# Attention and two expert layers: the second layer gathers quarter rows, and VectorE turns them in 32x32 blocks

## The chip, the cores and the metric

The kernel runs on one core of one Trainium2 chip. The metric is device time in microseconds (us) of one execution, as the median of three runs. TensorE (PE in the views) does the matrix products, VectorE (DVE), ScalarE (ACT) and GpSimd (POOL) the rest; SyncE (SP) issues most plain transfers, GpSimd issues the indirect ones (gathers and scatters by a table of row numbers).

## The reference

Three stages follow each other on N = 2304 tokens of D = 512 values: attention (4 batches, 8 heads, 576 positions, 64 values per head), a mixture of experts where each token goes to one of 8 experts, and a second one where each token goes to two. The second is the stage that is changed:

```python
def _moe2_ref(x, w_gate, w_noise, noise, w1, w2):
    logits = x @ w_gate
    noisy_logits = logits + np.log1p(np.exp(x @ w_noise)) * noise
    top2 = np.argpartition(-noisy_logits, 2, axis=1)[:, :2]
    ...                                  # top2_w: softmax over the two
    for e in range(E):                   # E = 8, w1[e] 512x1024, w2[e] 1024x512
        for k in range(2):
            mask = top2[:, k] == e
            out[mask] += top2_w[mask, k, None] * (np.maximum(x[mask] @ w1[e], 0.0) @ w2[e])
```

## The kernel before

Every fp32 product is made as three products of a rounded high part and a low part (high by high, high by low, low by high), so each matrix that is multiplied is first split: ScalarE casts the high part, VectorE subtracts it to get the low part. Attention and the first expert layer are put in order by a planner (queue `Q`); their last part and the second layer are written out in program order, which each engine follows.

**Layer 1 hands over through DRAM.** `x1_out` (line 871) writes each finished pair of 128-row blocks of layer 1's output to the table `xd` (520 values per row, 8 of them for routing). A few rows per expert that stay empty are filled with zeros during attention (`M.later`, line 1104).

**Layer 2** (`layer2`, line 967) begins at about 508 us. Each expert has 640 slots, in five tiles of 128 (the first 32 slots are always empty). Expert 0's first two tiles are done early, beside the end of the routing; its other three and then experts 1 to 7 follow, one expert per turn of the loop:

- *mm1* (lines 718 to 720): 8 blocks of hidden columns, each in two groups of 12 matmuls on 304 slots. ScalarE and VectorE turn each group into `hh` and `hl` (lines 721, 723), from two PSUM banks that alternate. In the same stretch `split_w` (693, 694) splits this expert's `w2`.
- *mm2* (lines 728 to 730): five output tiles, each in two half-calls of 12 matmuls with 512 columns. Between half-calls a list `todo` is worked off two entries at a time: eight splits of the next expert's `w1` (`split_w1`, 697, 698) and the five tiles of the next expert's input (`xsplit`, 705 to 710). `xsplit` turns a gathered tile with four TensorE transposes (708) into PSUM, casts `xh` from there (709) and subtracts for `xl` (710).
- *output* (`l2_out`, line 960): ScalarE scales the tile into `os` (963; two buffers that alternate), and a GpSimd scatter adds its rows to `out` in DRAM (964). Each scatter waits until the one before has landed, since both write `out`; ScalarE may write an `os` buffer again only when the scatter from it has landed.
- *loads*: at the top of an expert GpSimd issues five gathers of 128 rows of `xd` for the next expert (701, five buffers `gs`). SyncE loads the next `w2` when mm1 is over, and the `w1` after next when the last `split_w1` is done (690); each load is 2 MB.

Of the kernel before, what the change touches and what calls it, by code (L numbers as in the profile page):

```python
# [307 lines left out]
class Moe:  # L308
    def __init__(s, ctx, tc, ident, consts, areas):
# [40 lines left out]
    def blocks(s, nc, c, areas):  # L350

        def T(j, o, w, name, dt=FT):
            assert o+w<=AREAS[j]
# [4 lines left out]
        s.w1r=V(T(K0,0,4096,'w1r'),KD); s.w2r=V(T(K0,4096,4096,'w2r'),KF); s.os=cut(K0,8192,512,'os',2)
        s.w1h=V(T(K1,0,4096,'w1h',FR),KD); s.w1l=V(T(K1,4096,4096,'w1l',FR),KD); s.yt=V(T(K1,8192,1024,'yt'),KD); s.rr=c.tile([128,4,256],FR,name='rrm')
        s.xh=V(T(X,0,2560,'xh',FR),KD); s.xl=V(T(X,2560,2560,'xl',FR),KD)  # L360
        s.w2h=cut(W2,0,512,'w2h',KF,FR); s.w2l=cut(W2,4096,512,'w2l',KF,FR)
# [3 lines left out]
        s.wb1=V(T(W2,0,4096,'wb1'),KD); s.wb2=V(T(W2,4096,4096,'wb2'),KF)  # L365
        s.x1=V(T(X1,0,2*XW,'x1'),2); s.ol2=V(T(OL,0,512,'ol2',FR),4); s.gs=cut(G,0,XW,'gs',GB); s.gn_=s.on_=0
# [593 lines left out]
    def l2_out(s, wk, y, tb, c, out):  # L960
# [3 lines left out]
        nc.gpsimd.indirect_dma_start(out=out,out_offset=bass.IndirectOffsetOnAxis(ap=si[:,c:c+1],axis=0),in_=o,in_offset=None,compute_op=OP.add)  # L964
    def l2_gather(s, wk, tb, c, ts=range(T2)):
        return [s.gather(s.xd[:],tb[0][:,c+t:c+t+1]) for t in ts]
    def layer2(s, w1, w2, out):
# [7 lines left out]
        s.load_w(s.w1r,w1,E+1)  # L975
        s.chain=s.route2(wk,ps,NF+NP2,2); s.hold=0
        for f in range(KF):
            s.mm1(ps,f,DEAD,EARLY-DEAD)
            if f==1: s.behind()
            if f in LSLOT2: s.logits(wk,ps,1+LSLOT2.index(f))  # L980
            s.split_w(s.w2r,s.w2h,s.w2l,f,nc.vector if f in (3,5,7) else nc.gpsimd)
            if f>LSLOT2[2]: s.pump(f,GATE2,PUMP2)
        s.load_w(s.w2r,w2,E+1)
        for t in range(NE):
# [15 lines left out]
        for e in range(E):  # L1000
            nxt=e+1<E
            if nxt:
                if e: s.load_w(s.w1r,w1,E+e+1)
                g=s.l2_gather(wk,tb,(e+1)*TS)
            for f in range(KF):
# [8 lines left out]
            for t in range(T2): todo.insert(2*t+1,lambda t=t:s.xsplit(ps,g[t],t*128))
            n=-(-len(todo)//(2*len(ts)-1))
            for t in ts:
                for q in range(2):
                    y=s.mm2(ps,t*128,range(4*q,4*q+4),y if q else None)
                    if nxt:
                        for _ in range(n):  # L1020
                            if todo: todo.pop(0)()
# [55 lines left out]
def build(tc, q, k, v, mz, beta, ids, mbias, wg, w1, w2, wcat, noise, out):  # L1077
    nc = tc.nc
    with ExitStack() as ctx:
# [24 lines left out]
        M.later = [Q.add(100 * (5 + j // 5), SP, 1000, f, [A.sunk[4 + j // 5]]) for j, f in enumerate(dma)]  # L1104
# [51 lines left out]
```

## Time and profile before

| | us |
|---|---|
| median of three runs | 985.74 |
| lowest and highest run | 985.54, 986.47 |
| the profiled execution | 987.47 |
| span of its trace | 985.8 |
| TensorE busy | 946.3 |
| VectorE busy | 541.9 |
| ScalarE busy | 487.4 |
| GpSimd busy | 350.4 |

The profiled execution is one more run of the same program, so sums made from its rows start from 987.47, of which 1.67 lie outside the span. Busy shares are averages over three unlike stages; a stage's own rows say what limits it.

### The profile page before, as it was taken

The numbers are of one execution on the slowest core, as the hardware profiler recorded it, in microseconds if no ns is written. First come the engines' busy times: TensorE is split into PE (matmuls) and PEld (weight loads), VectorE is DVE, ScalarE is ACT, GpSimd is POOL, SyncE is SP. The second block draws the span as 40 slices with busy tenths as digits, with TensorE's granted clock in tenths as the row PEclk, the third lists the DMA queues.
The fourth block names the chain that finished last, engine by engine and source line by source line (L and its number), as shares of the span: only waits on it lengthen the run. The fifth ranks groups of instructions, "written<-read, shape, count | busy, mean of one in ns | idle before, by whom it ended". The sixth has DMA issues, their size and how long they took to land. (4 is left out here: it accounts for less than half of the span.)

```text
span 985.8 us, 18580 instructions
## 1 busy us (share of the span) xinstructions
PE 946.3 (96%) x6849; PEld 832.9 (84%) x6849; DVE 541.9 (55%) x1695; ACT 487.4 (49%) x1141; POOL 350.4 (36%) x411
## 2 busy tenths in 40 slices
PE   7999999999998999999988999999999999999994
PEld 5888888878875989888877999898989989898983
DVE  8777777888764667777755244243342424244310
ACT  6887878775433555555543243343342333334320
POOL 5222232244543667766744231121314021221111
PEclk9999999999999999999989999999999999999997
DMA  8336856261485655556654253536446354534212
GB/s 210 109 103 187 272 180 201 101 222 53 173 274 221 215 198 189 195 196 211 214 189 137 65 134 124 128 76 161 109 107 164 105 120 117 150 77 110 30 20 37
DMA packets 83841, 144.98 MB, mean 147 GB/s; under 512 B 14480, under 2 KB 32912, under 8 KB 83728
## 3 DMA queue, kind: packets, MB, share of 16 engines
q1 hardware_dynamic: 73168, 117.10, 36.1%
q0 software_dynamic: 10560, 26.47, 13.5%
q8 instruction: 60, 0.98, 0.4%
q14 instruction: 53, 0.43, 0.1%
HBM read 111.65 MB, written 31.97 MB: 146 GB/s over the span
## 5 line engine op out<-in xcount | busy, mean ns | idle before, releaser
L718 PE MATMUL b<-xh,w1h 128*128 128x304 f32 (+3 forms) x800 | 241.8, 302 | 6.2 <-ACTq L791 3.7
L719 PE MATMUL b<-xl,w1h 128*128 128x304 f32 (+3 forms) x800 | 239.4, 299 | 3.3 <-DVEq L786 3.1
L720 PE MATMUL b<-xh,w1l 128*128 128x304 f32 (+3 forms) x800 | 238.5, 298 | 0.0
L723 DVE SCALAR_TENSOR_TENSOR hl<-b,hh 128x304 fp32r<-128x304 f32 (+3 forms) x200 | 90.9, 454 | 232.7 <-ACT hh L721 227.2
L728 PE MATMUL b<-w2h,hh 128*128 128x512 f32 x464 | 187.8, 405 | 0.0
L730 PE MATMUL b<-w2h,hl 128*128 128x512 f32 x464 | 181.7, 392 | 0.0
L729 PE MATMUL b<-w2l,hh 128*128 128x512 f32 x464 | 181.0, 390 | 0.0
L964 POOL DMA_INDIRECT out_dram<-os,l2s x40 | 63.1, 1578 | 329.3 <-ACT os L963 256.2
L721 ACT ACTIVATE hh<-b 128x304 fp32r<-128x304 f32 (+3 forms) x200 | 81.8, 409 | 182.6 <-PE b L720 172.2
L718 PEld LDWEIGHTS b<-xh,w1h 128*128 128x128 f32 x800 | 154.1, 193 | 13.2 <-DVE hl L723 5.5
L719 PEld LDWEIGHTS b<-xl,w1h 128*128 128x128 f32 x800 | 154.3, 193 | 4.4 <-DVEq L786 3.3
L720 PEld LDWEIGHTS b<-xh,w1l 128*128 128x128 f32 x800 | 154.3, 193 | 0.0
L730 PEld LDWEIGHTS b<-w2h,hl 128*128 128x128 f32 x464 | 87.1, 188 | 19.5
L729 PEld LDWEIGHTS b<-w2l,hh 128*128 128x128 f32 x464 | 87.4, 188 | 15.6
L728 PEld LDWEIGHTS b<-w2h,hh 128*128 128x128 f32 x464 | 87.2, 188 | 15.4
L151 ACT ACTIVATE p<-sm,l 128x128 f32<-128x128 f32 (+4 forms) x144 | 84.1, 592 | 16.9 <-DVE l L147 16.9
L698 DVE TENSOR_TENSOR w1l<-w1r,w1h 128x512 fp32r<-128x512 f32 x84 | 67.9, 816 | 23.7 <-ACT w1h L697 23.5
L693 ACT CAST w2h<-w2r 128x512 fp32r<-128x512 f32 x128 | 78.5, 613 | 0.0
L710 DVE TENSOR_TENSOR xl<-b,xh 128x512 fp32r<-128x512 f32 x56 | 38.6, 689 | 71.9 <-ACT xh L709 71.9
L709 ACT CAST xh<-b 128x512 fp32r<-128x512 f32 x56 | 32.9, 587 | 89.6 <-PE b L708 89.5
L963 ACT ACTIVATE os<-b,l2w 128x512 f32<-128x512 f32 x40 | 27.7, 691 | 97.8 <-PE b L730 47.9
L697 ACT CAST w1h<-w1r 128x512 fp32r<-128x512 f32 x128 | 74.8, 620 | 0.0
(457 smaller groups left out, 1497.6 us busy)
## 6 DMA issues: line engine op xcount, KB each, us to landing
w1r<-in_w_dram SPq DMA_DIRECT2D x18, 2048.0 KB, 9.5
w2r<-in_w_dram SPq DMA_DIRECT2D x18, 2048.0 KB, 9.1
xd<-gs SPq DMA_DIRECT2D x24, 260.0 KB, 3.1
xd<-x SPq DMA_DIRECT2D x10, 520.0 KB, 10.8
out_dram<-gs SPq DMA_DIRECT2D x19, 256.0 KB, 2.6
k<-in_k_dram SPq DMA_DIRECT2D x16, 256.0 KB, 3.9
q<-in_q_dram SPq DMA_DIRECT2D x16, 256.0 KB, 3.2
v<-in_v_dram SPq DMA_DIRECT2D x16, 256.0 KB, 5.4
```

The lines of the kernel that those rows point to most:

```text
L151: s.nc.scalar.activation(s.P[b,i,u][:,lh*n:lh*n+n],s.SM[b,i,u][:,lh*n:lh*n+n],AF.Exp,scale=-1.0,bias=L[:,0,c:c+1],accum_out=L[:,1,c:c+1])
L693: nc.scalar.copy(hi[c],raw[:,c])
L697: nc.scalar.copy(s.w1h[:,:,fs],s.w1r[:,:,fs])
L698: eng.tensor_sub(s.w1l[:,:,fs],s.w1r[:,:,fs],s.w1h[:,:,fs].bitcast(FT))
L718: nc.tensor.matmul(h[:,:n],s.w1h[:,k,fs],s.xh[:,k,cs],start=k==0,stop=False)
L719: nc.tensor.matmul(h[:,:n],s.w1h[:,k,fs],s.xl[:,k,cs],start=False,stop=False)
L720: nc.tensor.matmul(h[:,:n],s.w1l[:,k,fs],s.xh[:,k,cs],start=False,stop=k==KD-1)
L721: def mm1_a(s, h, f, c0, n): s.nc.scalar.activation(s.hh[:,f,c0:c0+n],h[:,:n],AF.Relu)
L723: cs=slice(c0,c0+n); s.nc.vector.scalar_tensor_tensor(s.hl[:,f,cs],h[:,:n],0.0,s.hh[:,f,cs].bitcast(FT),op0=OP.max,op1=OP.subtract)
L728: nc.tensor.matmul(y,s.hh[:,f,cs],s.w2h[f],start=f==0,stop=False)
L729: nc.tensor.matmul(y,s.hh[:,f,cs],s.w2l[f],start=False,stop=False)
L730: nc.tensor.matmul(y,s.hl[:,f,cs],s.w2h[f],start=False,stop=f==KF-1)
```

## The change

Layer 1 writes its output twice: to `xd` as before, and to a new table `xq` that holds each row as four quarter rows of 128 values (512 bytes). The zero rows are written to `xq` too, 24 more transfers.

In layer 2, experts 1 to 7 fetch each tile with four gathers of 128 quarter rows instead of one gather of 128 whole rows, 140 gathers where there were 35. The four gathers place the quarters so that 32x32 blocks of one tile are all that has to be transposed: one VectorE block transpose (`bsplit`) turns it in SBUF, ScalarE casts from there, VectorE subtracts. The order of the 512 values that the product sums over becomes another, and `w1` of these experts is loaded in that order (`by='(p c)'`: 16 KB in one piece per partition, where it was four of 4 KB). The gathers are no longer issued together: those of tile 0 stand at the top of an expert, the others each behind a one-column copy (`pace`) that reads a result of mm1 (`hl`) or of a split (`w1l`). The order of the list `todo` changes too. A table of quarter row numbers is worked out once (`quarter_sel` on GpSimd, `quarter_tables` with four small matmuls and two VectorE steps). Expert 0 keeps whole rows and TensorE transposes.

```diff
+    def bsplit(s, g, c0):
+        nc=s.nc; x=s.xt_[s.xn%2]; s.xn+=1
+        nc.vector.transpose(x.rearrange('p j (s t) -> p s j t',s=4),g.rearrange('p (s d j) -> p s j d',s=4,j=KD))
+        nc.scalar.copy(s.xh[:,:,c0:c0+128],x)
+        nc.vector.tensor_sub(s.xl[:,:,c0:c0+128],x,s.xh[:,:,c0:c0+128].bitcast(FT))
...
-        s.nc.sync.dma_start(d[:,c:c+n] if isinstance(c,int) else d[:,bass.ds(c,n)],s.x1[:,:n])
+        for d,w in ((d,XW),(dq,D)): s.nc.sync.dma_start(d[:,c:c+n] if isinstance(c,int) else d[:,bass.ds(c,n)],s.x1[:,:n,:w])
...
+    def quarter_gather(s, c, t, behind=None):
+        if behind is not None: s.nc.gpsimd.tensor_copy(s.pace,behind.bitcast(FT))
+        for i in range(4):
+            s.nc.gpsimd.indirect_dma_start(out=s.gq[t][:,i*128:(i+1)*128],out_offset=None,in_=s.xq[:],in_offset=bass.IndirectOffsetOnAxis(ap=s.gq4[:,i,c+t:c+t+1],axis=0))
...
+            if f==5: s.quarter_sel()
...
+        s.quarter_tables()
         for t in range(NE,T2): s.xsplit(ps,ge[t-NE],t*128)
...
-                if e: s.load_w(s.w1r,w1,E+e+1)
-                g=s.l2_gather(wk,tb,(e+1)*TS)
+                if e: s.load_w(s.w1r,w1,E+e+1,by='(p c)')
+                s.quarter_gather((e+1)*TS,0)
...
+                at=(2,4,6) if not e else (3,6)
+                if nxt and f in at: s.quarter_gather((e+1)*TS,1+at.index(f),s.hl[:,f,C2-1:C2])
...
-            for t in range(T2): todo.insert(2*t+1,lambda t=t:s.xsplit(ps,g[t],t*128))
+            for t in range(T2): todo.insert(2*t+2 if t<4 else len(todo),lambda t=t:s.bsplit(s.gq[t],t*128))
+            later=[(0,4)] if not e else [(0,3),(2,4)]
...
+                        i=2*(t-ts[0])+q
+                        if later and i==later[0][0]: s.quarter_gather((e+1)*TS,later.pop(0)[1],s.w1l[:,0,(i+1)*128:(i+1)*128+1])
...
-        M.later = [Q.add(100 * (5 + j // 5), SP, 1000, f, [A.sunk[4 + j // 5]]) for j, f in enumerate(dma)]
+            dma.append(lambda r=r: nc.sync.dma_start(M.xq[4 * (r - N):4 * (r - N) + 512].rearrange('(p q) d -> p (q d)', q=4), zt[:, :D]))
+        M.later = [Q.add(100 * (5 + j // 7), SP, 1000, f, [A.sunk[4 + j // 7]]) for j, f in enumerate(dma)]
```

**GpSimd's order** around the mm2 of expert 1, before: the five gathers for expert 2 (`gs`) stand together at the top, and behind them expert 1's five scatters (`os`).

```order
L701 DMA gs_98<-xd,l2g 128x520
L701 DMA gs_99<-xd,l2g 128x520
L701 DMA gs_100<-xd,l2g 128x520
L701 DMA gs_96<-xd,l2g 128x520
L701 DMA gs_97<-xd,l2g 128x520
L964 DMA out_dram<-os_61,l2s 2432x512
L964 DMA out_dram<-os_62,l2s 2432x512
L964 DMA out_dram<-os_61,l2s 2432x512
```

The same piece of the changed kernel, from the gathers of tile 0 to the second scatter.

```order
L992 DMA gq_94<-xq,gq_8406 128x128 x4
L990 COPY pace<-hl_88 128x1
L992 DMA gq_95<-xq,gq_8406 128x128 x4
L990 COPY pace<-hl_88 128x1
L992 DMA gq_96<-xq,gq_8406 128x128 x4
L990 COPY pace<-w1l 128x1
L992 DMA gq_97<-xq,gq_8406 128x128 x4
L973 DMA out_dram<-os_61,l2s 2432x512
L990 COPY pace<-w1l 128x1
L992 DMA gq_98<-xq,gq_8406 128x128 x4
L973 DMA out_dram<-os_62,l2s 2432x512
```

Twenty gathers stand where five stood; those of tile 3 now stand ahead of the first scatter, and those of tile 4 ahead of the second.

**ScalarE's order** in the same mm2 from the first output tile (`os_61`, tile 0) to the last, before: the last cast of a `w1` piece stands behind the third `os`.

```order
L963 ACTIVATE os_61<-b_158,l2w 128x512
L697 CAST w1h<-w1r 128x4x128
L709 CAST xh<-b_159 128x4x128
L697 CAST w1h<-w1r 128x4x128
L709 CAST xh<-b_160 128x4x128
L963 ACTIVATE os_62<-b_157,l2w 128x512
L697 CAST w1h<-w1r 128x4x128
L709 CAST xh<-b_159 128x4x128
L697 CAST w1h<-w1r 128x4x128 x2
L963 ACTIVATE os_61<-b_158,l2w 128x512
L697 CAST w1h<-w1r 128x4x128
L963 ACTIVATE os_62<-b_157,l2w 128x512
```

The same piece of the changed kernel; `xtq` is the tile that VectorE has turned.

```order
L972 ACTIVATE os_61<-b_167,l2w 128x512
L711 CAST xh<-xtq_99 128x4x128
L699 CAST w1h<-w1r 128x4x128
L711 CAST xh<-xtq_100 128x4x128
L699 CAST w1h<-w1r 128x4x128
L972 ACTIVATE os_62<-b_166,l2w 128x512
L711 CAST xh<-xtq_99 128x4x128
L699 CAST w1h<-w1r 128x4x128 x3
L972 ACTIVATE os_61<-b_167,l2w 128x512
L711 CAST xh<-xtq_100 128x4x128
L972 ACTIVATE os_62<-b_166,l2w 128x512
L972 ACTIVATE os_61<-b_167,l2w 128x512
```

The last `w1` cast has moved ahead of the third `os` (it stood behind it), and the casts of the x tiles no longer read a PSUM bank that TensorE wrote.

**TensorE's order** at the first gap between half-calls of that mm2, before: the four transposes of a tile (`ident`, `gs`) stand between two half-calls. Five such rows per expert are gone from the changed kernel, 35 in all.

```order
L728 MATMUL b_158<-w2h_72,hh_87 128x512
L729 MATMUL b_158<-w2l_80,hh_87 128x512
L730 MATMUL b_158<-w2h_72,hl_88 128x512
L708 MATMUL b_159<-ident,gs_98 128x128 x4
L728 MATMUL b_158<-w2h_73,hh_87 128x512
```

In the changed kernel the last row follows the third directly.

## Rows read from the trace of the kernel before

**Rows 1.** The page's first part: busy time, share of the span, instructions.

```profile
PE 946.3 (96%) x6849; PEld 832.9 (84%) x6849; DVE 541.9 (55%) x1695; ACT 487.4 (49%) x1141; POOL 350.4 (36%) x411
```

**Rows 2.** Windows: length, PE, PEld, DVE, ACT, POOL busy, PEclk, DMA share, GB/s.

```profile
750.00:800.00 50.00, 50.00 (x304) 45.75 (x303) 21.77 (x37) 19.78 (x41) 11.80 (x10) 1.00 0.44 99
...
135.00:145.00 10.00, 10.00 (x111) 7.99 (x109) 7.62 (x30) 8.31 (x22) 3.01 (x3) 1.00 1.04 369
```

**Rows 3.** Timeline of TensorE, 662 to 720: start, length, what [idle before it].

```profile
662.39 0.39 PE L728 MATMUL b<-w2h,hh 128*128 128x512 f32 x1
...
678.35 0.47 PE L728 MATMUL b<-w2h,hh 128*128 128x512 f32 x1
...
692.06 0.30 PE L718 MATMUL b<-xh,w1h 128*128 128x304 f32 x1
...
719.43 0.39 PE L728 MATMUL b<-w2h,hh 128*128 128x512 f32 x1
```

**Rows 4.** Groups by line, 530 to 986: busy, mean ns | idle before, releasers.

```profile
L964 POOL DMA_INDIRECT out_dram<-os,l2s x40 | 63.1, 1578 | 329.3 <-ACT os L963 256.2 <-issue 52.3 <-DMA out_dram<-os,l2s 16.4
...
L698 DVE TENSOR_TENSOR w1l<-w1r,w1h 128x512 fp32r<-128x512 f32 x56 | 37.9, 687 | 14.6 <-ACT w1h L697 14.4
L697 ACT CAST w1h<-w1r 128x512 fp32r<-128x512 f32 x56 | 34.0, 620 | 0.0
...
L710 DVE TENSOR_TENSOR xl<-b,xh 128x512 fp32r<-128x512 f32 x38 | 26.3, 691 | 65.7 <-ACT xh L709 65.7
L708 PE MATMUL b<-ident,gs 128*128 128x128 f32 x152 | 22.7, 272 | 0.9 <-DVE xl L710 0.7 <-DMA gs<-xd,l2g 0.2
```

**Rows 5.** Timeline of GpSimd, 670 to 703: two scatters, then gathers.

```profile
682.45 1.55 POOL L964 DMA_INDIRECT out_dram<-os,l2s  x1 [3.99 <-ACT os L963]
692.14 1.56 POOL L964 DMA_INDIRECT out_dram<-os,l2s  x1 [8.14 <-issue]
697.66 1.55 POOL L964 DMA_INDIRECT out_dram<-os,l2s  x1 [3.96 <-issue]
...
700.85 0.98 POOL L701 DMA_INDIRECT gs<-xd,l2g  x1 [0.30 <-PE b L720]
702.13 0.95 POOL L701 DMA_INDIRECT gs<-xd,l2g  x1 [0.30 <-issue]
```

**Rows 6.** Tile gs, its gathers: shortest, median and longest ns, first and last.

```profile
L701 POOL DMA_INDIRECT gs<-xd,l2g x38: 942/948/1466, 533.5 to 874.4; - x38
```

**Rows 7.** Timeline, 682 to 695, of SyncE's queue, ScalarE and VectorE.

```profile
683.38 0.37 SPq L690 DMA_DIRECT2D w1r<-in_w_dram  x1
...
682.66 0.69 DVE L698 TENSOR_TENSOR w1l<-w1r,w1h 128x512 fp32r<-128x512 f32 x1 [1.52 <-ACT w1h L697]
...
692.31 0.69 ACT L963 ACTIVATE os<-b,l2w 128x512 f32<-128x512 f32 x1 [4.75 <-PE b L730]
693.94 0.42 ACT L721 ACTIVATE hh<-b 128x304 fp32r<-128x304 f32 x1 [0.94 <-PE b L720]
...
694.40 0.47 DVE L723 SCALAR_TENSOR_TENSOR hl<-b,hh 128x304 fp32r<-128x304 f32 x1 [11.04 <-ACT hh L721]
```

**Rows 8.** Timeline at experts 0 and 1: mm2's start, scatters, a load.

```profile
559.99 0.39 PE L728 MATMUL b<-w2h,hh 128*128 128x512 f32 x1
...
575.91 1.58 POOL L964 DMA_INDIRECT out_dram<-os,l2s  x1 [5.25 <-ACT os L963]
...
576.89 0.37 SPq L690 DMA_DIRECT2D w1r<-in_w_dram  x1
...
625.91 1.55 POOL L964 DMA_INDIRECT out_dram<-os,l2s  x1 [4.06 <-ACT os L963]
636.05 1.55 POOL L964 DMA_INDIRECT out_dram<-os,l2s  x1 [8.59 <-issue]
```

**Rows 9.** DMA issues on the page: KB each, median us from issue to landing.

```profile
w1r<-in_w_dram SPq DMA_DIRECT2D x18, 2048.0 KB, 9.5
xd<-x SPq DMA_DIRECT2D x10, 520.0 KB, 10.8
```

More of the change, by code (lines that the diff above doesn't have):

```diff
@@ L313, in __init__ @@
         s.dram=ctx.enter_context(tc.tile_pool(name='dram',bufs=1,space=bass.MemoryType.DRAM))
+        s.xq=s.dram.tile([4*SLOTS,D//4],FT,name='xq')
         s.xd=s.dram.tile([N+SLOTS,XW],FT,name='xd')
@@ L365, in blocks @@
         s.wb1=V(T(W2,0,4096,'wb1'),KD); s.wb2=V(T(W2,4096,4096,'wb2'),KF)
+        s.gq=cut(G,0,D,'gq',GB); s.xt_=[V(t,KD) for t in cut(X1,0,D,'xtq',2)]; s.xn=0; s.sel4=V(T(K1,8192,512,'sel4',FR),4); s.sel4f=V(T(K1,8704,512,'sel4f'),4)
         s.x1=V(T(X1,0,2*XW,'x1'),2); s.ol2=V(T(OL,0,512,'ol2',FR),4); s.gs=cut(G,0,XW,'gs',GB); s.gn_=s.on_=0
@@ L686, in tasks, with load_w @@
         Q.add(P+14,POOL,300,lambda:nc.gpsimd.memset(s.rr[:,:,4*NC2:].bitcast(FT),0.0))
-    def load_w(s, raw, w, e, eng=None):
-        src=(w[bass.ds(e,1)] if not isinstance(e,int) else w[e:e+1]).rearrange('o (c p) f -> p (o c) f',p=128)
+    def load_w(s, raw, w, e, eng=None, by='(c p)'):
+        src=(w[bass.ds(e,1)] if not isinstance(e,int) else w[e:e+1]).rearrange('o %s f -> p (o c) f'%by,p=128)
         (eng or s.nc.sync).dma_start(raw,src)
@@ L704, in o, with xsplit @@
         s.on_+=1; return s.os[s.on_%2]
-    def xsplit(s, ps, g, c0):
+    def bsplit(s, g, c0):
[3 more added lines that the diff above has]
+        nc.vector.tensor_sub(s.xl[:,:,c0:c0+128],x,s.xh[:,:,c0:c0+128].bitcast(FT))
+    def xsplit(s, ps, g, c0, fourth=False):
         nc=s.nc
         tp=ps.tile([128,KD,128],FT,name='tp')
-        for k in range(KD): nc.tensor.transpose(tp[:,k],g[:,k*128:(k+1)*128],s.ident)
+        for k in range(KD): nc.tensor.transpose(tp[:,k],g[:,k:D:4] if fourth else g[:,k*128:(k+1)*128],s.ident)
         nc.scalar.copy(s.xh[:,:,c0:c0+128],tp)
@@ L736, in state @@
         nc=s.nc; c=s.c
+        s.qn=c.tile([128,1],FT,name='qn'); s.pace=c.tile([128,1],FT,name='pace')
         s.run=c.tile([128,E],FT,name='run'); nc.gpsimd.memset(s.run,float(DEAD))
@@ L964, in l2_out, with quarter_sel, quarter_tables @@
         nc.gpsimd.indirect_dma_start(out=out,out_offset=bass.IndirectOffsetOnAxis(ap=si[:,c:c+1],axis=0),in_=o,in_offset=None,compute_op=OP.add)
+    def quarter_sel(s):
+        G=s.nc.gpsimd; f=s.sel4f
+        G.memset(f,0.0)
+        G.affine_select(f.rearrange('p s (g t) -> p s g t',g=4),f.rearrange('p s (g t) -> p s g t',g=4),pattern=[[-32,4],[0,4],[-1,32]],compare_op=OP.not_equal,fill=1.0,base=0,channel_multiplier=1)
+        G.tensor_copy(s.sel4,f)
+        for g in range(4): G.memset(s.qn[32*g:32*g+32],float(g))
+    def quarter_tables(s):
+        nc=s.nc; V=nc.vector; m=s.c.tile([128,NC2],FR,name='mq'); f=s.c.tile([128,4,NC2],FT,name='fq'); s.gq4=s.c.tile([128,4,NC2],I32,name='gq4')
+        V.tensor_copy(m,s.M2[:,0])
+        p=s.ps.tile([128,512],FT,name='sm')
+        for i in range(4): nc.tensor.matmul(p[:,i*NC2:(i+1)*NC2],s.sel4[:,i],m,start=True,stop=True)
+        V.tensor_scalar(f,p[:,:4*NC2].rearrange('p (s c) -> p s c',s=4),float(S0),0.0,op0=OP.add,op1=OP.max)
+        V.tensor_scalar(s.gq4,f,4.0,s.qn[:,0:1],op0=OP.mult,op1=OP.add)
+    def quarter_gather(s, c, t, behind=None):
+        if behind is not None: s.nc.gpsimd.tensor_copy(s.pace,behind.bitcast(FT))
+        for i in range(4):
+            s.nc.gpsimd.indirect_dma_start(out=s.gq[t][:,i*128:(i+1)*128],out_offset=None,in_=s.xq[:],in_offset=bass.IndirectOffsetOnAxis(ap=s.gq4[:,i,c+t:c+t+1],axis=0))
     def l2_gather(s, wk, tb, c, ts=range(T2)):
@@ L974, in layer2 @@
         s.x1_out(s.nf*2+(FC-4),2)
-        s.load_w(s.w1r,w1,E+1)
+        s.load_w(s.w1r,w1,E+1,by='(p c)')
         s.chain=s.route2(wk,ps,NF+NP2,2); s.hold=0
@@ L1066, in overflow @@
                 e=nc.values_load(ov[0:1,o:o+1],engines=[ET.SP],min_val=0,max_val=E-1)
-                s.load_w(s.w1r,w1,e+E); s.load_w(s.w2r,w2,e+E)
+                s.load_w(s.w1r,w1,e+E,by='(p c)'); s.load_w(s.w2r,w2,e+E)
                 for ff in range(KF): s.split_w1(ff,nc.vector)
-                for t,g in enumerate(s.l2_gather(wk,tb,o*T2)): s.xsplit(ps,g,t*128)
+                for t,g in enumerate(s.l2_gather(wk,tb,o*T2)): s.xsplit(ps,g,t*128,True)
                 for ff in range(KF):
```

2 lines of the change are left out of this document (1 added, 1 removed).

## The prediction

> **What bounds the kernel now.** I read the page's busy shares first: TensorE is busy 96% of the span, no other engine above 55% [rows 1]. A share of the whole span can hide a stage, so the windows come next. In layer 2 TensorE is busy 50.00 of 50 us at a granted clock of 1.00 (2.4 GHz), VectorE 21.77, ScalarE 19.78, GpSimd 11.80, the DMA engines 0.44 of their time [rows 2]. So in the changed stage only TensorE's own time counts, until something makes it wait. Then I read TensorE's timeline over one expert: mm2 from 662.39 to 692.06, mm1 from there to 719.43 [rows 3]. The reader is to see two things: mm2 takes 29.67 us, and its last five half-calls, with no transposes between, take 692.06 - 678.35 = 13.71 us, or 2.742 each.
>
> **What is removed.** Ten half-calls at 2.742 us are 27.42, so the five groups of four transposes cost 29.67 - 27.42 = 2.25 us per expert, 0.45 a group. The group of lines gives 272 ns for one transpose [rows 4], 1.09 for four; that they overlap each other and the matmuls behind them is why the difference of the timeline is used instead. Seven experts lose them: 7 x 2.25 = 15.7 us, with TensorE never idle around them.
>
> **What VectorE, ScalarE and GpSimd get instead.** 35 block transposes of 128x512. The trace has none; the nearest row is VectorE's subtraction of the same shape, 0.69 us [rows 4]. Bounds: half and twice that. Even 1.4 us makes 7 us on VectorE per expert of 54.8, where it is idle 28 of 50 us [rows 2]; hidden. The cast of `xh` from SBUF in place of PSUM is taken at the `w1` cast's 0.62 us [rows 4]; hidden too. What hides both is that an x tile is needed only in the next mm1, at least 7 us after the last tile is turned; without that cover it would be some 2 us per expert.
>
> GpSimd gets 20 gathers per expert in place of five. A gather of 128 whole rows occupies it 0.95 us and the next starts 1.28 us after (700.85 to 702.13), about 1.25 at the median [rows 5, 6]. A quarter gather moves a quarter of the bytes in as many pieces. Bounds from issue to issue: by bytes alone 0.95/4 + 0.30 = 0.54; by the longest gather of the trace, 1.47 + 0.30 = 1.77 [rows 6]. I take 1.25, since the number of pieces is the same. Twenty are then 25 us, five scatters 8 [rows 4], the copies 1: 34 of 54.5 us. Not full, but they now lie among the scatters.
>
> A rule speaks against this. The Trainium skill, "DMA: Bandwidth & Descriptors", section "Anatomy of one DMA — SWDGE (gpsimd) path", fits a GpSimd-issued transfer as about 2.0 us plus its bytes at 436 GB/s, and "Rules for kernel authors" asks to coalesce small ones. If that were time during which the next must wait, an estimate of 20 x 2.15 + 9 = 52 us would nearly fill GpSimd's expert. The trace does not bear that reading out: gathers of 266 KB follow each other every 1.25 us.
>
> **What is moved, and what becomes late.** I call T the start of mm2 of an expert (662.39 above), mm2 now 27.42 long. Three orders matter.
>
> *The load of w1.* It is issued the moment the last `w1` split is subtracted: 682.66 + 0.69 ends at 683.35, the load is at 683.38, or T+21.0 [rows 7]. By the new order that cast stands ahead of the third `os`. The second `os` can start at T+11.0 (four half-calls) and behind it one x cast and three `w1` casts of 0.6 follow, then a subtraction; the work of a half-call ahead of them pushes this to about T+15.3. So the load starts at T+15.4, one output tile earlier.
>
> *The scatters.* Undisturbed, one scatter follows the other after 5.5 us (692.14 to 697.66). The one beside which the load is issued takes 9.7 (682.45 to 692.14), which is 8.8 after the load's issue [rows 5, 7]; at the longest of the six loads of this kind it is 10.1 [rows 8]. So far it is the third scatter. In the new order GpSimd has tile 2's gathers until T+3.1, tile 3's until T+8.3, the first scatter at T+8.5, tile 4's gathers from T+10.5 to T+15.4, the second scatter at T+15.6. It is now this second one that meets the load. By the load's issue it lands at T+24.2, by its own at T+25.3; I take T+24.6. The third starts then and lands at T+30.1.
>
> *The last os.* Its buffer is the third tile's, so ScalarE cannot write it before T+30.1, where mm2's end would allow T+27.7 (692.31 less 2.25, less T). Behind it in ScalarE's order stands `hh` of the next mm1's first group: at T+30.75 in place of T+29.3 (693.94 less 2.25, less T), and `hl` ends about 0.95 later [rows 7], at T+31.7. The third group of mm1 needs that PSUM bank, two groups of 1.7 (27.37/16) after mm2, at T+30.8. TensorE waits about 1.0 us. The delay of `os` is 2.4, of which 1.4 is slack. Bounds: above 2.1, with the longest pair, 10.1 in place of 9.0; below, nothing, where quarter gathers are faster than taken: at under 1.0 us the second scatter starts by T+12.7, ahead of the load, and the third is not held up so far. This is at experts 1 to 5, 5 x 1.0 = 5.0 us. At expert 0 mm2 has three tiles (16.45 us); its load moves from T+16.9 (576.89, behind the second scatter at 575.91; mm2 from 559.99) [rows 8] to about T+10.7, three us behind the first scatter at T+7.7. If that scatter waits for the load's end, 8.8 later, the third `os` is at T+19.5 in place of 16.7, less the slack 1.4: 1.4 us; bounds 0 and 1.4, and I take the upper, since in the trace no scatter beside a load escaped. Expert 6 has no load behind it. Sum of waits: 6.4 us, bounds 0 and 12.
>
> **The tables.** Four matmuls of 48 columns stand on TensorE ahead of expert 0's transposes: 0.4 us, bounds 0 and 1.1 (four transposes in sequence [rows 4]). GpSimd's part lies beside the early tiles, where it waits; nothing, or 3 us if it were late for the gathers.
>
> **Attention and layer 1.** 24 zero transfers and some 17 of 512 KB are added, about 15 MB to the 145. In the worst window the DMA engines are at 1.04 and TensorE is still busy 10.00 of 10 [rows 2]: loads are ahead of their use. The nearest row for one write is 10.8 us to land [rows 9], and a pair of blocks is rewritten some 19 us later. I take 0, bounds 0 and 2. The longer pieces of the `w1` load could shorten its 9.5 us [rows 9]; what that would save is below the waits' bound.
>
> **The sum**, against the profiled execution: 987.47 - 15.7 + 6.4 + 0.4 = 978.6. The median lies 1.73 below that execution, so about **977 us**.
>
> **The rivals.**
> *A, no waits at the boundaries.* Quarter gathers under 1.0 us, or a scatter that does not slow beside the load. 977 - 6.4 = 970.5. For it: the bytes are a quarter. Against it: the gathers' time is nearly constant at 942 to 948 in most of them, which looks like a cost per piece [rows 6].
> *C, longer waits.* Above 1.4 us of slack every us of delay of the last `os` is one at six boundaries. If scatters queue behind 512 pieces of a tile's gathers and land 1 to 2 us later, it is 983 to 989. For it: both go through one queue. Against it: in the trace a scatter behind nothing and the fourth scatter take the same 5.5.
> *D, slower: GpSimd issues too slowly.* The second scatter's start is T-1.9 + 12 gathers + one scatter (1.6). While it starts before T+19 it lands with the load at T+24.6; behind that, each 0.1 us more per gather is 1.2 us at six boundaries. From 1.72 us per gather the gain is gone (970.5 + 6 x 2.5 = 985.7 with 2.5 us of wait each). At the longest gather seen, 1.77: second scatter T+20.9, third lands T+31.9, wait 2.8, 970.5 + 17 = 987.5. For it: VectorE's subtraction for `xl` now reads SBUF twice, and gathers of up to 1.47 us occur in the trace. Against it: the median is 0.95.
> *E, the skill's rule as occupancy.* At 2.0 us per gather the second scatter starts at T+23.7, the third lands at T+34.7, the wait is 5.6 us, and the time 970.5 + 34 = 1004. The rule of "DMA: Bandwidth & Descriptors" above would give a little more. No row shows such a step.
>
> **How the numbers follow.** The forecast 0.47, with a range of its own from 974 to 981; A 0.30; C 0.12 (half of it under 985); D 0.08; E 0.03. Two thousandths, or 2 us, is what a measurement of this kernel can tell from no change. Faster: forecast, A and half of C, 0.82; same, between 984 and 988: 0.08; slower: 0.10. The range from 969 to 985 leaves out A's lowest, half of C, D and E, about 0.2.
>
> **What the changed profile would show.** No group of TensorE on the tile `gs` in experts 1 to 7, and mm2 of 27.4 us. Gathers on `gq` of 0.95 us at steps of 1.25. The load of `w1` about 15 us into mm2, and behind it the second, not the third scatter with a gap of 9 us. A wait of TensorE of about 1 us at the third group of mm1 of experts 2 to 6, released by `hl`, and a last `os` 30 us after T. I am wrong if gathers take over 1.7 us, if TensorE waits in attention where it did not, if a turned tile is late so that mm1's start waits for `xl`, or if the boundaries show no wait at all.

## The result, and the profile after

The changed kernel takes 997.91 us (median of 4 runs, 994.25 to 1002.07) against 986.11 before (four runs, one more than in the table above): a ratio of 1.0132, 95% interval 1.011 to 1.0155. It is slower by 1.3 percent; 977 was predicted. Before, the runs lay within 1.1 us of each other; now they spread over 8. The profiled execution is the slowest of the four, 1002.07, with a span of 1000.4; what is read from its rows is 4.2 us above the median.

The page's first part for the changed kernel, and windows of its layer 2 (columns as in [rows 2]):

```profile
PE 942.4 (94%) x6713; PEld 831.0 (83%) x6713; DVE 578.0 (58%) x1733; ACT 489.1 (49%) x1141; POOL 472.7 (47%) x551
```

```profile
700.00:750.00 50.00, 49.91 (x274) 45.79 (x275) 24.34 (x40) 18.45 (x38) 27.50 (x28) 0.94 0.48 126
750.00:800.00 50.00, 46.33 (x273) 42.95 (x272) 25.13 (x40) 20.12 (x41) 25.93 (x26) 0.97 0.40 91
800.00:850.00 50.00, 46.81 (x270) 43.59 (x269) 19.19 (x34) 15.97 (x33) 21.79 (x22) 0.93 0.41 99
```

Where 50.00 of 50 us were busy at a clock of 1.00 [rows 2], TensorE now stands still for up to 3.7 us in a window, and its granted clock falls. TensorE's timeline shows where (the bracket is the idle time ahead of a matmul and what ended it):

```profile
640.33 0.41 PE L726 MATMUL b<-xh,w1h 128*128 128x304 f32 x1 [3.21 <-DVE hl L731]
...
665.31 0.39 PE L736 MATMUL b<-w2h,hh 128*128 128x512 f32 x1
...
692.53 0.30 PE L726 MATMUL b<-xh,w1h 128*128 128x304 f32 x1
...
700.09 0.62 PE L726 MATMUL b<-xh,w1h 128*128 128x304 f32 x1 [4.05 <-DVE hl L731]
...
725.97 0.39 PE L736 MATMUL b<-w2h,hh 128*128 128x512 f32 x1
...
760.37 0.62 PE L726 MATMUL b<-xh,w1h 128*128 128x304 f32 x1 [3.67 <-DVE hl L731]
...
819.13 0.62 PE L726 MATMUL b<-xh,w1h 128*128 128x304 f32 x1 [3.19 <-DVE hl L731]
...
879.72 0.62 PE L726 MATMUL b<-xh,w1h 128*128 128x304 f32 x1 [3.79 <-DVE hl L731]
```

Five waits, one at the start of mm1 of each of experts 2 to 6, for `hl`, 17.9 us together; a sixth, of 0.50, follows expert 0 (in the mm1 of expert 1). The mm2 from 665.31 to 692.53 takes 27.22 us, where it took 29.67 [rows 3]: the transposes are gone and worth 2.45 an expert. But the mm1 behind it takes 33.44 (692.53 to 725.97) where it took 27.37: 4.05 of that is the wait, and most of the rest is a slower TensorE behind it. Windows of that stretch show the clock:

```profile
692.00:696.00 4.00, 4.00 (x28) 3.67 (x26) 0.69 (x1) 0.84 (x2) 1.57 (x1) 1.00 0.17 9
696.00:700.05 4.05, 0.03 (x1) 0.00 (x0) 0.47 (x1) 1.53 (x4) 0.86 (x1) 0.83 0.39 57
700.05:704.00 3.95, 3.92 (x15) 3.92 (x16) 1.09 (x3) 0.78 (x3) 0.69 (x1) 0.50 0.54 66
704.00:708.00 4.00, 4.00 (x25) 4.00 (x25) 1.63 (x3) 1.03 (x3) 2.87 (x2) 0.81 0.28 17
```

TensorE was at 1.00 (2.4 GHz), idled 4.05 us, and then ran at 0.50 (1.2 GHz) for some 5 us: 15 matmuls in 3.95 us where 28 went into 4.00. An mm1 without a wait takes 26.67 us in this trace (expert 7, from 931.86 to 958.53). Over the five boundaries mm1 takes 28.8 us more than five times that, of which the waits are 17.9; the other 10.9 are, for the most part, this.

Now the chain of the wait at 700.09, from the timelines of GpSimd, SyncE's queue, VectorE and ScalarE; T, the start of mm2, is 665.31:

```profile
663.99 0.96 POOL L992 DMA_INDIRECT gq<-xq,gq  x1 [0.50 <-issue]
...
666.63 1.35 POOL L992 DMA_INDIRECT gq<-xq,gq  x1 [0.30 <-issue]
...
675.49 1.62 POOL L973 DMA_INDIRECT out_dram<-os,l2s  x1 [0.31 <-issue]
...
681.52 0.94 POOL L992 DMA_INDIRECT gq<-xq,gq  x1 [0.30 <-issue]
682.77 1.63 POOL L973 DMA_INDIRECT out_dram<-os,l2s  x1 [0.30 <-ACT os L972]
693.60 1.57 POOL L973 DMA_INDIRECT out_dram<-os,l2s  x1 [9.21 <-ACT os L972]
```

```profile
681.63 0.34 SPq L692 DMA_DIRECT2D w1r<-in_w_dram  x1
...
690.42 1.08 DVE L710 STREAM_TRANSPOSE xtq<-gq 128x512 f32<-128x512 f32 x1 [8.82 <-DMA gq<-xq,gq]
692.18 0.69 DVE L712 TENSOR_TENSOR xl<-xtq,xh 128x512 fp32r<-128x512 f32 x1 [0.69 <-ACT xh L711]
...
692.91 0.69 ACT L972 ACTIVATE os<-b,l2w 128x512 f32<-128x512 f32 x1 [0.76 <-DMA out_dram<-os,l2s]
698.52 0.69 ACT L972 ACTIVATE os<-b,l2w 128x512 f32<-128x512 f32 x1 [4.92 <-DMA out_dram<-os,l2s]
699.11 0.42 ACT L729 ACTIVATE hh<-b 128x304 fp32r<-128x304 f32 x1
```

The load of `w1` is issued at T+16.3, in the middle of mm2, and the second scatter (T+17.5) stands beside it: the third follows only 10.83 us later, and the last `os` waits for the third's landing until T+33.2. That is the chain of the prediction, link by link, but later by 3 us. This boundary is the worst of the five; over all five the third scatter follows after 9.9 to 10.8 us and the last `os` starts at T+32.4 to T+33.2, 32.7 in the mean. The load holds up more than the scatter: the last gather of tile 4, issued at 681.52 just ahead of it, lets VectorE begin only at 690.42.

The whole difference of the two profiled executions, 14.6 us, in stages (start of mm2 of expert 0, 1, 6, 7; from the timelines): up to expert 0's mm2 2.35 later; expert 0 1.75 faster; experts 1 to 5 298.23 in place of 283.06, 15.17 slower; expert 6, behind which no load stands, 53.90 in place of 56.33; the end some 1.3 longer.

### The profile page after: what moved, and what is told of

It reads as the page before. It is cut to its first block, busy times and chain, and to the rows that moved or that the text cites. A ratio compares the mean times of both kernels' runs of the same rounds, so it can differ in the third digit from the quotient of the medians.

```text
span 1000.4 us, 18441 instructions
## 1 busy us (share of the span) xinstructions
PE 942.4 (94%) x6713; PEld 831.0 (83%) x6713; DVE 578.0 (58%) x1733; ACT 489.1 (49%) x1141; POOL 472.7 (47%) x551
## 5 line engine op out<-in xcount | busy, mean ns | idle before, releaser
L726 PE MATMUL b<-xh,w1h 128*128 128x304 f32 (+3 forms) x800 | 246.1, 308 | 24.0 <-DVE hl L731 18.6
L727 PE MATMUL b<-xl,w1h 128*128 128x304 f32 (+3 forms) x800 | 243.2, 304 | 3.2 <-DVEq L795 2.9
L728 PE MATMUL b<-xh,w1l 128*128 128x304 f32 (+3 forms) x800 | 242.3, 303 | 0.0
L736 PE MATMUL b<-w2h,hh 128*128 128x512 f32 x464 | 185.7, 400 | 0.0
L726 PEld LDWEIGHTS b<-xh,w1h 128*128 128x128 f32 x800 | 157.8, 197 | 31.5 <-DVE hl L731 23.6
L992 POOL DMA_INDIRECT gq<-xq,gq x140 | 147.0, 1050 | 42.7 <-issue 41.5
L727 PEld LDWEIGHTS b<-xl,w1h 128*128 128x128 f32 x800 | 157.8, 197 | 4.4 <-DVEq L795 3.1
L728 PEld LDWEIGHTS b<-xh,w1l 128*128 128x128 f32 x800 | 157.6, 197 | 0.0
L696 POOL TENSOR_TENSOR w2l<-w2r,w2h 128x512 fp32r<-128x512 f32 x45 | 58.3, 1304 | 35.6 <-ACT w2h L695 35.4
L700 POOL TENSOR_TENSOR w1l<-w1r,w1h 128x512 fp32r<-128x512 f32 x44 | 57.6, 1318 | 33.8 <-ACT w1h L699 33.7
```

The lines of the kernel that those rows point to most:

```text
L700: eng.tensor_sub(s.w1l[:,:,fs],s.w1r[:,:,fs],s.w1h[:,:,fs].bitcast(FT))
L726: nc.tensor.matmul(h[:,:n],s.w1h[:,k,fs],s.xh[:,k,cs],start=k==0,stop=False)
L727: nc.tensor.matmul(h[:,:n],s.w1h[:,k,fs],s.xl[:,k,cs],start=False,stop=False)
L728: nc.tensor.matmul(h[:,:n],s.w1l[:,k,fs],s.xh[:,k,cs],start=False,stop=k==KD-1)
L736: nc.tensor.matmul(y,s.hh[:,f,cs],s.w2h[f],start=f==0,stop=False)
L992: s.nc.gpsimd.indirect_dma_start(out=s.gq[t][:,i*128:(i+1)*128],out_offset=None,in_=s.xq[:],in_offset=bass.IndirectOffsetOnAxis(ap=s.gq4[: ...
```

## The experiments

Three theories were set against each other. W: the load of `w1`, moved one output tile ahead, meets the second scatter, and the last `os` comes late. Its first rival, G: GpSimd's queue is too full with twenty gathers, wherever the load stands. X: VectorE's new work is the cost.

**Four os buffers.**

```diff
-s.os=cut(K0,8192,512,'os',2)
+s.os=cut(K0,8192,512,'os',2)+cut(K1,8192,512,'osx',2)
-        s.on_+=1; return s.os[s.on_%2]
+        s.on_+=1; return s.os[(s.on_-1)%4]
```

> The changed kernel with four os buffers in place of two, so that ScalarE may write the fifth tile without waiting for the third tile's scatter. Theory W (the third scatter lands late, since the second one meets the load of w1; that holds the last os, hh, hl and so TensorE's third group of mm1): the waits of 3.2 to 4.1 us at five experts go, the granted clock there stays 1.00, and of the 998 us some 18 of waits and 8 of low clock are saved: 972 (968 to 978). Rival G (GpSimd's own queue is full: twenty gathers and five landings in order do not fit in an expert, so a turned tile or a scatter is late whatever os does): the wait moves to another place and the time stays above 985.

Measured: 993.47 us (992.13 to 997.58), ratio 1.0061 to before (1.0044 to 1.0078). The waits at the third group went, as W says: experts 1 to 5 took 286.50 us in the profiled execution, in place of 298.23. But the time missed the expected 972 by 21 us: others of 2.3 us stand at the end of mm1 of four experts, where GpSimd, late by its scatters, issues eight gathers in a row, and expert 0's mm2 took 24.3 us in this execution, in place of 16.4. Neither theory as stated; G is nearer.

**All gathers together.**

```diff
-                s.quarter_gather((e+1)*TS,0)
+                for t in range(T2): s.quarter_gather((e+1)*TS,t)
...
-                if nxt and f in at: s.quarter_gather((e+1)*TS,1+at.index(f),s.hl[:,f,C2-1:C2])
...
-            later=[(0,4)] if not e else [(0,3),(2,4)]
...
-                        if later and i==later[0][0]: s.quarter_gather((e+1)*TS,later.pop(0)[1],s.w1l[:,0,(i+1)*128:(i+1)*128+1])
```

> The changed kernel with all twenty quarter gathers of an expert issued together at its top, no pacing copies. Theory W: GpSimd is then free when the first output tile is ready; the first scatter starts about 8.5 us into mm2 where it was 10.2, the second about 14 where it was 17.5, the third lands at about 29.7 where it was 33; the wait of TensorE falls from 3.6 to about 0.6 us an expert, and the time to 975 to 981. Rival G (the number of gathers is the cost, wherever they stand): no fall below 990. Rival X (VectorE's transposes or its subtraction with two SBUF operands slow the boundary): no change from 998.

Measured: 1089.71 us (1082.78 to 1094.41), ratio 1.1017 (1.0972 to 1.1062). A miss by over 100 us, and not G as I had meant it either: GpSimd keeps its step of 1.25 us and is done in 25. It is the other engines that stop. Windows of this kernel across one row of gathers (605.14 to 630.5 us; columns as in [rows 2]):

```profile
605.00:610.00 5.00, 5.00 (x38) 5.00 (x37) 2.74 (x5) 2.29 (x5) 3.94 (x4) 1.00 0.58 92
610.00:615.00 5.00, 5.00 (x37) 4.79 (x35) 1.71 (x4) 1.36 (x3) 3.78 (x5) 1.00 0.17 43
615.00:620.00 5.00, 2.53 (x13) 2.49 (x12) 0.47 (x1) 0.42 (x1) 3.78 (x5) 0.82 0.20 54
620.00:625.00 5.00, 2.88 (x12) 2.51 (x12) 1.17 (x2) 0.93 (x2) 3.78 (x5) 0.50 0.20 53
625.00:630.00 5.00, 0.92 (x4) 0.55 (x3) 0.00 (x0) 0.00 (x0) 3.78 (x5) 0.50 0.19 51
630.00:635.00 5.00, 0.56 (x2) 0.57 (x3) 1.09 (x3) 1.24 (x3) 0.46 (x1) 0.50 0.08 22
```

Five gathers to a window throughout, the DMA engines busy 0.2, and TensorE, ScalarE and VectorE run down to nothing or nearly so within 20 us; ScalarE starts again 3 us after the last gather, at 633.45. Up to 611.75 each `hh` starts 0.04 us after its group's last matmul is over; the next are 3.2, 6.5 and 13.0 late. I call this theory S: a long row of gathers holds up what passes between the other engines.

**Whole rows, turned by VectorE.**

```diff
-                s.quarter_gather((e+1)*TS,0)
+                g=s.l2_gather(wk,tb,(e+1)*TS)
...
-                if nxt and f in at: s.quarter_gather((e+1)*TS,1+at.index(f),s.hl[:,f,C2-1:C2])
...
-            for t in range(T2): todo.insert(2*t+2 if t<4 else len(todo),lambda t=t:s.bsplit(s.gq[t],t*128))
-            later=[(0,4)] if not e else [(0,3),(2,4)]
+            for t in range(T2): todo.insert(2*t+2 if t<4 else len(todo),lambda t=t:s.bsplit(g[t][:,:D],t*128))
...
-                        if later and i==later[0][0]: s.quarter_gather((e+1)*TS,later.pop(0)[1],s.w1l[:,0,(i+1)*128:(i+1)*128+1])
```

> The changed kernel with five gathers of whole rows at the top of an expert in place of twenty of quarter rows; VectorE turns those tiles in 32x32 blocks as before, which leaves the values of a tile in other places, so the products of experts 1 to 7 are taken on reordered inputs. Theory W: the load of w1 still comes one tile early, but the scatters start on time: third landing near 29.7 us into mm2, a wait of about 0.6, 974 to 981. Rival X (VectorE's transposes are the cost): stays near 998. Beside the kernel with the gathers together it shows what 105 more gathers cost by their number alone: nothing by W, several us an expert by G.

Measured: 973.62 us (972.91 to 974.65), ratio 0.9862 (0.9846 to 0.9879), as W expected, and 24 us less than the changed kernel. X falls: every block transpose, every subtraction with two SBUF operands and the early load are in it, and over layer 2 (560 us on) its list of waits has no more than this of TensorE for `hl`:

```profile
PE b L726 <- DVE hl L731: 0.3, 1, 0.3
```

So the loss needs the gathers: 140 in place of 35, for nearly the same bytes. How they make it is seen in the timelines of GpSimd, SyncE's queue and ScalarE in the mm2 that begins at T = 661.52:

```profile
673.92 1.58 POOL L973 DMA_INDIRECT out_dram<-os,l2s  x1 [4.09 <-ACT os L972]
677.13 0.34 SPq L692 DMA_DIRECT2D w1r<-in_w_dram  x1
679.60 1.87 POOL L973 DMA_INDIRECT out_dram<-os,l2s  x1 [4.09 <-ACT xh L711]
...
689.00 0.69 ACT L972 ACTIVATE os<-b,l2w 128x512 f32<-128x512 f32 x1 [4.75 <-PE b L738]
```

The load is as early as in the changed kernel (T+15.6), but no gathers stand ahead of the scatters, and the second one starts at T+12.4, three us before the load. It is the third that meets it, as before the change, and the last `os` waits for TensorE alone (T+27.5). The early load does harm only together with scatters that come late.

**No loads of w1.**

```diff
-                if e: s.load_w(s.w1r,w1,E+e+1,by='(p c)')
```

> The changed kernel with the six loads of w1 of experts 2 to 7 left out (these experts work with the weights of an earlier one). Theory W: the second scatter starts 17.5 us into mm2 as in the changed kernel but lands 5.5 us after, at 23, the third at 28.5; the last os is then not late beyond its slack of 1.4 us, TensorE does not wait, and the time is 970 to 976. If the lateness comes from the gathers and their pacing alone, without the load: waits of 2 us or more stay, above 985.

Measured: 981.44 us (979.48 to 984.47), ratio 0.9942 (0.9924 to 0.9961). It is 5 us over the expected 970 to 976; expert 0's mm2 alone took 8 us more than in the changed kernel (24.46 in place of 16.36, see theory S); from expert 1 to 6 an expert takes 53.9, one of them 54.9, with no wait for `hl` at all. GpSimd's and ScalarE's timelines in the mm2 that begins at T = 669.10:

```profile
686.57 1.63 POOL L973 DMA_INDIRECT out_dram<-os,l2s  x1 [0.30 <-issue]
692.19 1.57 POOL L973 DMA_INDIRECT out_dram<-os,l2s  x1 [4.00 <-ACT os L972]
...
697.09 0.69 ACT L972 ACTIVATE os<-b,l2w 128x512 f32<-128x512 f32 x1 [4.89 <-DMA out_dram<-os,l2s]
```

The second scatter starts at T+17.5, as in the changed kernel, but the third follows after 5.62 us and not 10.83, and the last `os` is at T+28.0 and not 33.2. W holds for the waits between experts. (The last `os` comes some half us late here and still causes no wait: that is within the slack.)

**The load late, nothing left out.**

```diff
-                if e: s.load_w(s.w1r,w1,E+e+1,by='(p c)')
...
+                if e and f==3:
+                    s.split_w1(KF-1,nc.vector)
+                    if nxt: s.load_w(s.w1r,w1,E+e+1,by='(p c)')
...
-            todo=[(lambda f=f:s.split_w1(f,nc.vector)) for f in range(KF)]
+            todo=[(lambda f=f:s.split_w1(f,nc.vector)) for f in range(KF-1)]
```

> The changed kernel with the split of the last eighth of w1 moved out of mm2 into the next mm1, behind its fourth block (that eighth is needed only by the eighth block), so that the load of the next w1, which waits for that split, starts about 11 us into mm1 and not 16 us into mm2. Nothing is left out. Theory W (the load beside the second scatter makes the last os late): the experts run at 53.9 us each as in the kernel without these loads, no wait at mm1's third group, 977 to 985. If what the kernel without loads won was DMA traffic as such and not its place: waits come back elsewhere, above 990.

Measured: 983.23 us (981.68 to 987.56), ratio 0.9963 (0.9943 to 0.9983). Within what W expected: the same bytes, moved from the second scatter into mm1, save 14.7 us between the medians of the two sessions, and it is now a little faster than before the change. What is left is mostly expert 0 again, whose mm2 took 24.7 (one other expert has waits of 2.3 us); TensorE's waits there end by nothing that the profile shows, and its windows are:

```profile
560.00:575.00 15.00, 10.77 (x47) 8.24 (x45) 7.92 (x11) 4.29 (x8) 11.76 (x13) 0.97 0.16 48
575.00:590.00 15.00, 14.17 (x64) 12.28 (x64) 7.04 (x10) 6.47 (x12) 3.19 (x2) 0.80 0.28 39
```

Sixteen gathers stand there from 553.1 to 574.5, parted only by copies whose sources are long done. But such a row does not always stop TensorE. The changed kernel has the same sixteen from 554.0 to 576.0, and in its profiled execution TensorE is busy throughout, at a clock of 1.00:

```profile
554.00:576.00 22.00, 22.00 (x111) 19.62 (x110) 12.26 (x18) 8.51 (x16) 17.82 (x19) 1.00 0.17 46
```

**Twenty, and ten, gathers in a row in the kernel before.** Its edit, with 4 or 2 for n:

```diff
-                g=s.l2_gather(wk,tb,(e+1)*TS)
+                for _ in range(n): g=s.l2_gather(wk,tb,(e+1)*TS)
```

> The kernel before, but its five whole-row gathers of an expert are issued four times over into the same five buffers: 20 gathers in a row at the top of an expert, nothing else changed, the result too. Theory S (a long unbroken row of gathers holds up the signals from TensorE to ScalarE, as in the kernel with all gathers together, whatever they fetch): waits of several us in mm1 appear, above 1030. If the quarter rows, their turning or the order of the changed kernel made those waits: within 6 of 987.

> The kernel before with its five gathers issued twice over: 10 in a row. Theory S with a limit somewhere above five (five in a row gave one pause of about 1 us in the trace of before, 20 gave 8 to 12): a few us an expert, 995 to 1020. Without theory S: within 4 of 987.

Measured: 1115.38 us (1110.71 to 1121.52), ratio 1.1291 (1.1235 to 1.1348), and 1029.36 (1027.78 to 1033.44), ratio 1.0431 (1.0397 to 1.0466), the second above what I expected. Nothing of the change is in these, neither quarter rows nor VectorE's transposes; 15 more whole-row gathers an expert cost 18 us an expert, 5 more cost 6. S holds for unbroken rows of ten and twenty. ScalarE's and TensorE's waits over layer 2 (560 us on) of the kernel with twenty (engine, tile, line, what ended the wait: us in all, times, longest):

```profile
ACT hh L721 <- remote: 90.5, 12, 12.3
...
PE b L718 <- issue: 54.4, 12, 8.7
```

"remote" is a signal whose sender the profile can't name, "issue" a wait for nothing that it shows. ScalarE's timeline in the kernel with ten, whose gathers run from 656.01 to 668.3:

```profile
660.19 0.42 ACT L721 ACTIVATE hh<-b 128x304 fp32r<-128x304 f32 x1 [1.25 <-issue]
...
663.22 0.42 ACT L721 ACTIVATE hh<-b 128x304 fp32r<-128x304 f32 x1 [2.10 <-PE b L720]
668.23 0.42 ACT L721 ACTIVATE hh<-b 128x304 fp32r<-128x304 f32 x1 [4.58 <-remote]
```

The first `hh` that is late (by 1.4 us) comes after the sixth gather has begun, the next is 4.7 late.

**The writes of the second table alone.** The kernel before with the lines of the change that write `xq` in attention and layer 1:

```diff
+        for d,w in ((d,XW),(dq,D)): s.nc.sync.dma_start(d[:,c:c+n] if isinstance(c,int) else d[:,bass.ds(c,n)],s.x1[:,:n,:w])
```

> The kernel before with the writes of the second table alone (the zero rows in attention, 512 KB behind each pair of blocks in layer 1), which nobody reads; layer 2 is as before. My prediction put these at 0 (bounds 0 and 2): 986 to 988. If traffic in attention and layer 1 is part of the loss: 990 or more.

Measured: 988.64 us (987.39 to 991.64) against 987.28 in the same session, ratio 1.0013 (0.9999 to 1.0026). At most 2.6 us by the interval, perhaps nothing; it is no large part of the loss.

**Together.** The late load; expert 1's tiles, their order in `todo` and its `w1` as before the change; the tables of quarter rows beside expert 0's mm1:

```diff
-                s.quarter_gather((e+1)*TS,0)
+                if e: s.quarter_gather((e+1)*TS,0)
+                else: g=s.l2_gather(wk,tb,TS)
...
-                at=(2,4,6) if not e else (3,6)
+                at=() if not e else (3,6)
...
-            if f==5: s.quarter_sel()
-        s.quarter_tables()
...
+                    if f==2: s.quarter_sel()
+                    if f==6: s.quarter_tables()
```

> The changed kernel with the late load of w1, and with expert 1's tiles fetched and turned as before the change (five whole rows, TensorE transposes), so that no row of sixteen gathers lies beside expert 0; the tables of quarter rows are worked out beside expert 0's mm1 and not ahead of its transposes. Nothing is left out. By theories W and S together: experts 1 to 6 run at 53.9 us each where before they took 56.3 to 57.0, expert 0 as before: 971 to 976. If a row of gathers or a load still meets something: 980 or more.

Measured: 972.96 us (972.11 to 975.06), ratio 0.9861 (0.9839 to 0.9883). As expected, and faster than both kernels. One window, and the load against the scatters, in that kernel:

```profile
650.00:700.00 50.00, 50.00 (x286) 45.30 (x285) 23.96 (x38) 19.19 (x38) 27.11 (x27) 1.00 0.51 132
```

```profile
677.57 1.63 POOL L973 DMA_INDIRECT out_dram<-os,l2s  x1 [0.30 <-issue]
683.21 1.56 POOL L973 DMA_INDIRECT out_dram<-os,l2s  x1 [4.01 <-ACT os L972]
688.59 1.55 POOL L973 DMA_INDIRECT out_dram<-os,l2s  x1 [3.82 <-issue]
...
702.79 0.34 SPq L692 DMA_DIRECT2D w1r<-in_w_dram  x1
```

TensorE is never idle in it, these scatters follow at 5.4 to 5.6 us, and the load comes when the scatters are over. The second scatter still starts at T+17.2 (T is 660.35), as late as in the changed kernel. G falls with this run too: experts 2 to 7 have their twenty quarter gathers each, and experts 1 to 6 take 53.9 us each.

**The same with four os buffers.**

> The same with four os buffers. Theory W says that with the load out of the way the last os is no longer late beyond its slack: within 2 us of the kernel with two buffers. If the os buffers still hold something: 3 us or more faster.

Measured: 973.78 us (971.17 to 976.51), ratio 0.9873 (0.9847 to 0.9898); no difference to the last that can be told. With the load out of the way the `os` buffers hold nothing up, as W says.

**The changed kernel with expert 1 as before, the load still early.** The edits for expert 1 above, without the late load and with the tables where the change has them.

> The changed kernel as it is, with the load of w1 in its early place, but with expert 1's tiles as before the change (five whole rows, TensorE transposes, no pacing in expert 0). Theory S: the sixteen gathers beside expert 0 cost about 8 us in the executions in which they hold TensorE up and nothing in others, so about 2 to 8 us less than 998, 990 to 996, and a smaller spread. If that row of gathers costs nothing: 998 to 1000.

Measured: 1004.07 us (1002.38 to 1010.39), ratio 1.019 (1.0149 to 1.0231). A miss: 6 us more than the changed kernel between the medians, where 2 to 8 less was expected (the two profiled executions, 1002.91 and 1002.07, hardly differ). Expert 0's mm2 did take 18.7, as before the change, but its second scatter now meets the load, also as before the change, and what is late there makes a row of gathers for expert 2:

```profile
577.82 1.57 POOL L973 DMA_INDIRECT out_dram<-os,l2s  x1 [5.24 <-ACT os L972]
588.74 1.56 POOL L973 DMA_INDIRECT out_dram<-os,l2s  x1 [9.35 <-DVE hl L731]
...
578.80 0.34 SPq L692 DMA_DIRECT2D w1r<-in_w_dram  x1
```

Eight gathers then follow from 590.61 to 600.8 with no pause between, and mm1 takes 29.2. The five later waits are there as in the changed kernel (2.7 to 4.0). So a late scatter can make a row of gathers, and one edit alone could not be priced as I had priced it. Nor did the spread shrink: the four runs still lie 8 us apart, without the row of sixteen.

## Why the prediction was wrong

**What is removed** was right: 2.25 an expert was predicted, 2.45 measured; 973 us is reached where nothing else stands in the way.

**VectorE's transposes** take 1.08 us each, within the bounds (0.35 to 1.4), and are hidden, but not by the cover that was named. An x tile was to be ready at least 7 us before its use. Tile 4, whose gathers met the load as well, was subtracted only by T+27.6 (692.18 + 0.69), after mm1 had begun at T+27.2. TensorE did not wait for it, since mm1's first group of 304 slots does not read that tile; the second group began 1.3 us later.

**The step that failed is "Sum of waits: 6.4 us, bounds 0 and 12".** The waits were 18.4 us: 17.9 at the five boundaries where 5.0 was taken, and 0.5 behind expert 0 where 1.4 was. The mechanism, the load beside the second scatter and the buffer of the third tile, was right in every link: without the load, and with a late one, the waits at mm1's third group go, and with the scatters early they go too. Its size was not right. In the boundary shown above the last `os` came at T+33.2 and not T+30.1. Of these 3.1 us, 1.9 were there when the second scatter began (T+17.5 for 15.6): gathers in mm2 step by 1.25 to 1.7 us and not by 1.25 throughout, and a pace copy from `w1l` takes 0.2 to 0.9 us. The pair beside the load added 1.8 (10.8 and not 9.0, above even the 10.1 that was the longest in the trace before), and the third scatter landed 0.6 sooner than taken. Since the slack was used up, the delay became TensorE's in full: over the five boundaries the last `os` is 2.6 us later than taken in the mean, and TensorE's wait is 3.6 and not 1.0. The text of rival C said so ("every us of delay of the last `os` is one at six boundaries") and gave it too little weight and too low an end.

At expert 0 the premise "in the trace no scatter beside a load escaped" did not carry over: its first scatter began 2.0 us ahead of the load (576.27, load at 578.23) and the next followed after 5.8.

**What the sum had no term for** is the clock. After an idle time of 3.2 to 4.1 us TensorE came back at 0.50, which with what else mm1 lost cost 10.9 us more over the five experts, some 60% on top of the waits. With these two the account nearly closes. Between the sum, 978.6, and the profiled execution lie 23.5 us. The waits are 12.0 of them, and the slower mm1 9.5 (10.9, of which the trace before had 1.4 already). The stretch ahead of expert 0's mm2 is 1.9 beyond its term, the end 1.3; the transposes gave 1.3 more than taken.

**A cost that was looked for in one place only.** I priced a gather by what it costs GpSimd (1.25 us, 34 of 54.5 us an expert, "not full") and looked for harm in GpSimd's queue alone. The runs show a cost that is not on GpSimd (theory S): ten in a row cost 6 us an expert, twenty 18. In the changed kernel the pace copies break most rows. Where they find their source done, as beside expert 0, the row is sixteen long, and expert 0's mm2 takes 24 to 25 us in the profiled executions of three kernels; in that of the changed kernel itself it takes 16.4. So beside expert 0 this cost is no part of the 23.5 us. Nor does it explain the spread of 8 us: the profiled execution, without it, is the slowest of the four. Where the spread comes from stays open.

**The rule that spoke against the change.** The Trainium skill, "DMA: Bandwidth & Descriptors", section "Rules for kernel authors", asks to coalesce many small transfers into one large one. One pair of runs agrees in effect: 973.62 us with 35 gathers, 997.91 with 140 of nearly the same bytes. The last runs do not: 972.96 us with 120 quarter gathers, once the load stands elsewhere. The other reading, that each gather holds GpSimd for the 2.0 us of the fit in the section "Anatomy of one DMA — SWDGE (gpsimd) path", did not come true: the step was 1.25 to 1.7 us.

**Attention and layer 1** cost 0 to 2.6 us, about as forecast. The writes were fewer than counted: ten of 512 KB and not 17. The tables ahead of expert 0 can't be told apart: without a long row of gathers ahead of it, the start of expert 0's mm2 lay between 559.8 and 564.2 us in the profiled executions of kernels with and without them.

## What to carry to other kernels

When a step is cheapened on the engine that bounds, follow what its neighbours in the order pull forward and push back: here a 2 MB load came one tile earlier, the dependent scatters came later behind new gathers, and the two met one scatter too soon. Either alone did no harm; with one eighth of a split moved, and the load behind it, it costs nothing. A wait that has used up its slack is paid in full from there on, several times over in a loop, and here on TensorE again in clock (0.50 after waits of 3.2 to 4.1 us); so a slack of a microsecond, worked out from steps that vary by half of one, should not carry a forecast. Gathers issued by GpSimd are to be counted in rows, and not only by their time on GpSimd: keep rows short and put work between them that really waits.

## What the runs showed of the hardware that was not expected

Long rows of indirect gathers of 128 pieces, 1.25 us apart, can hold up the other engines. In the kernel with ten in a row `hh`, which takes TensorE's result to ScalarE, is 1.4 us late from about the sixth on; in a row of twenty it is up to 13 us late. It happens with pieces of 512 bytes and the DMA engines 0.2 busy, and with pieces of 2080 bytes and the DMA engines 0.73 busy (615 to 620 us in the kernel before with twenty). The trace before held a trace of it: in a row of five one `hh` (706.68 us) started 1.1 us late. It does not happen always: a row of sixteen, broken by short copies, left TensorE busy 22.00 of 22 us in one kernel and cost some 8 us in three. Which resource is shared there the runs don't say; it was not separated whether it is the signals, the instruction supply or something else, and that stays open.

A scatter beside which a 2 MB load is issued is followed by the next, which waits for its landing, only after 9.2 to 10.8 us in the kernel before and the changed one, where it otherwise takes 5.4 to 6.1; one that began 2.0 us ahead of the load was followed after 5.8. A gather beside the load is held up too: one issued at 681.52 let its reader start only at 690.42.

A VectorE transpose of 128x512 fp32 in 32x32 blocks takes 1.08 us, where a subtraction of that shape takes 0.69.
